# Transposed accumulation for two token tiles of a gated spectral / key-lookup kernel, gate dots later, one more level of minima, a new order

## The chip, the core and the metric

One NeuronCore of a Trainium2 chip runs the kernel. The metric is device microseconds of one launch, the median of a few runs. The engines are TensorE (PE, with its weight loads PEld), VectorE (DVE), ScalarE (ACT), GpSimd (POOL) and the queue of SyncE (SP). All of them share 16 DMA engines.

## What is computed

The input x has 2048 tokens of 576 numbers. Branch a is a spectral filter: a 2-D real FFT, a product with a complex weight, the inverse FFT. Branch b picks, for each token and each of 32 heads, one row out of 4096 by the best of two 64-key scores, and adds up 32 weighted rows of v. A sigmoid gate mixes them.

```python
q  = einsum("nd,dhc->nhc", x, w_q)              # 32 heads, 2*128 numbers
i1 = argmax(q1 @ k1.T); i2 = argmax(q2 @ k2.T)  # 64 keys each, K = 1
e  = i1 * 64 + i2                               # row of u and v, 0..4095
g  = softmax over one candidate                 # = 1
act = gelu(einsum("nd,nhkd->nhk", x, u[e]))
b  = einsum("nhk,nhk,nhkd->nd", g, act, v[e])   # sum of 32 scaled v rows
a  = irfft2(rfft2(x) * (w_r + 1j * w_i))
gate = sigmoid((x * gate_w).sum(-1))
out = gate * a + (1 - gate) * b
```

## The kernel before, in words

The tokens are 16 tiles of 128. The heads are 8 chunks of 4. For each chunk `build_m` (line 335) folds w_q with the keys into a matrix of 512 columns, held in a high and a low part. `scores` (line 362) multiplies it with two token tiles at a time: 28 passes of 128x512 on PE for a pair of tiles, 224 for a chunk, 1792 in all. From the scores in PSUM, DVE takes the maximum of each group of 64 (line 385), ACT makes a sign of every score against its maximum (line 392, 16 instructions for a pair of tiles), and DVE finds the first hit by a tree of minima over bf16 numbers (lines 405, 413, 414) and a last reduction over 16 (line 416). The row number of a token and head goes to `ei` or `eil`.

The first ten tiles (`E_T`, 0 to 9) are worked by `group(t, c)` (line 458). It issues four gathers on POOL (line 465), each of 128 rows of 1152 numbers, u and v side by side, into a buffer `uv`. DVE makes the dot of x and u (line 472), ACT the gelu (line 474), and the factors `a` come from ACT (line 480) or DVE (line 483). The four scaled v rows are then summed in one of these ways, which the table `ROWS` chooses:

- DVE multiplies and adds into the sum `xn` (line 498);
- ACT scales the row in place (line 493), DVE adds it (line 494);
- the whole group goes to PE (an entry of 16): ACT makes four diagonal matrices `dg` (line 508), PE multiplies each with a v row in two halves of 288 columns (line 512), and DVE adds the sum from PSUM (line 522) or ACT copies it (line 520).

The other six tiles (10 to 15) are worked by `quad(t, c)` (line 543) after the last score: their gathers are at line 549, their dots at line 554, and their sums are made on PE with 32-column diagonals. They wait for the score of chunk 7 by `HELD`.

Branch a starts near the end of the scores: `fold` (line 688), then `unit` (line 822) with its twiddle tables from `turns` (line 719), then `invert`, and `mix` (line 868), which adds (1 - gate) times the sum. The gate's dots (`gates`, line 326) stand in two places: those of the first ten tiles near the start, with a copy of gate_w that `spread` (line 588) brings to all partitions by two matmuls, and those of the other six in `close_gates` (line 832), which then makes the sigmoid.

A gather needs a free `uv` buffer. There are 12, and others that come free later: one in `area`, and four `pair` buffers, which hold the x tiles 0 to 7 of the first ten two by two, and become `uv` buffers when the last reader of both x tiles is done (`plan.late`). Four PSUM buffers of two banks (`bank`) go round among scores, `build_m`, diagonal sums and the rest.

Nothing is scheduled by the machine: each piece of work is a job, the list `ORDER` at the end of the file gives the sequence of all jobs, and each engine executes its own in that sequence. An engine whose next job has to wait holds up all that stand behind it.

## Time and profile before

| | |
|---|---|
| median of 3 runs | 894.05 us (890.72 to 895.09) |
| the profiled execution | 895.22 us, its span 893.5 us |
| busy in the span | PE 852.5, PEld 652.8, DVE 822.3, ACT 597.2, POOL 579.5 us |
| moved by DMA | 342.41 MB, of which 302.02 MB are the gathers |
| mean granted TensorE clock | 0.984 |

The profiled execution took 1.7 us more than its span, and 1.2 us more than the median. A busy PE in these views is not PE at its peak, since matmuls overlap; the distance from one start to the next says more. The chain that ended last is the sequence of work that leads back from the last instruction to what released each step.

### The profile page before, as it was taken

The page shows a single profiled execution, that of the slowest core. Times are in us where ns is not written, and L with a number is a line of the kernel's source. Part 1 is how long each engine was busy: PE and PEld are TensorE (multiplying, and loading weights), DVE is VectorE, ACT ScalarE, POOL GpSimd, SP SyncE. Part 2 cuts the span into 40 slices and gives each one's busy share as a digit, 9 for nine tenths or more (in the row PEclk, how much of TensorE's full clock was granted, in tenths as well). Part 3 has the DMA queues.
Part 4 walks back from the last instruction along what each step waited for, and adds up shares of the span by engine and source line. Part 5 has one row for each costly group of instructions (what it writes and reads, how often), then busy time and mean ns, then how long its engine had stood idle before and what let it go on. Part 6 is the DMA issues. An engine that isn't in the chain of part 4 may idle for free.

```text
span 893.5 us, 16499 instructions
## 1 busy us (share of the span) xinstructions
PE 852.5 (95%) x5306; PEld 652.8 (73%) x5306; DVE 822.3 (92%) x2000; ACT 597.2 (67%) x2100; POOL 579.5 (65%) x516
## 2 busy tenths in 40 slices
...
GB/s 301 362 333 407 379 362 363 332 374 382 366 375 393 374 387 357 386 384 367 334 377 364 418 387 371 412 370 416 414 405 415 420 418 419 420 421 419 420 419 305
DMA packets 89611, 342.41 MB, mean 383 GB/s; under 512 B 9970, under 2 KB 10866, under 8 KB 89524
## 3 DMA queue, kind: packets, MB, share of 16 engines
q0 software_dynamic: 73728, 302.02, 86.5%
...
## 4 chain that ended last, share of the span: by engine, by line
PE 61%; DVE 22%; DMA 8%; ACT 5%; issue 3%; POOL 1%; DVEq 0%; SPq 0%; POOLq 0%; ACTq 0%
PE bank L256 61%; DVE uv L472 7%; DMA uv<-uv,ei 4%; DVE xn L498 3%; DVE xn L494 2%; DMA uv<-uv,eiq 2%; DVE area L385 2%; DVE uv L554 2%; ACT area L392 1%; DMA pair<-uv,eiq 1%; ACT uv L493 1%; POOL uv L465 1%; DVE area L405 1%; DVE pair L554 1%; DVE xn L522 0%
## 5 line engine op out<-in xcount | busy, mean ns | idle before, releaser
L465 POOL DMA_INDIRECT uv<-uv,ei x317 | 363.5, 1147 | 214.4 <-issue 44.7
L256 PE MATMUL bank<-mh,xt 128*128 128x512 f32 x768 | 263.3, 398 | 0.0
L392 ACT ACTIVATE area<-bank,area 128x64 bf16<-128x64 f32 x1024 | 222.7, 355 | 21.4 <-DVE area L385 14.4
L472 DVE SCALAR_TENSOR_TENSOR uv<-uv,pair 128x576 f32<-128x576 f32 x254 | 185.8, 751 | 7.9 <-DMA uv<-uv,ei 7.7
L549 POOL DMA_INDIRECT uv<-uv,eiq x136 | 150.3, 1105 | 57.7 <-issue 21.9
L256 PE MATMUL bank<-ml,xt 128*128 128x512 f32 x448 | 174.8, 390 | 0.0
L256 PEld LDWEIGHTS bank<-mh,xt 128*128 128x128 f32 x768 | 144.2, 188 | 31.2 <-ACT area L392 0.3
L256 PE MATMUL bank<-uv,dg 128*32 128x288 f32 (+2 forms) x868 | 146.3, 417 | 14.3 <-DVE dg L558 6.2
L256 PE MATMUL bank<-mhx,xt 128*128 128x512 f32 x384 | 135.2, 400 | 0.0
L256 PEld LDWEIGHTS bank<-uv,dg 128*32 128x32 f32 (+2 forms) x868 | 81.9, 141 | 51.5 <-issue 10.8
L554 DVE SCALAR_TENSOR_TENSOR uv<-uv,xr 128x576 f32<-128x576 f32 x136 | 99.9, 753 | 13.8 <-DMA uv<-uv,eiq 10.7
L256 PE MATMUL bank<-fi,bt 128*128 128x289 f32 x384 | 102.5, 418 | 3.0 <-ACT t L866 1.5
L498 DVE SCALAR_TENSOR_TENSOR xn<-uv,a,xn 128x576 f32<-128x576 f32 x124 | 100.0, 810 | 0.0
L256 PEld LDWEIGHTS bank<-fi,bt 128*128 128x128 f32 x384 | 83.0, 243 | 23.3 <-issue 5.8
L256 PEld LDWEIGHTS bank<-ml,xt 128*128 128x128 f32 x448 | 84.2, 188 | 16.5
L493 ACT ACTIVATE uv<-uv,a 128x576 f32<-128x576 f32 x103 | 77.6, 779 | 12.0 <-DVE a L483 11.8
L256 PEld LDWEIGHTS bank<-mhx,xt 128*128 128x128 f32 x384 | 72.2, 188 | 16.2 <-ACT area L392 0.3
L385 DVE TENSOR_REDUCE area<-bank 128x16 f32<-128x1024 f32 x64 | 77.6, 1216 | 1.5 <-PE bank L256 1.4
L494 DVE TENSOR_TENSOR xn<-uv,xn 128x576 f32<-128x576 f32 x103 | 77.2, 751 | 0.7 <-ACT uv L493 0.7
L256 PE MATMUL bank<-mlx,xt 128*128 128x512 f32 x192 | 74.9, 390 | 0.0
L400 ACT ACTIVATE area<-area 128x256 bf16<-128x256 bf16 x192 | 71.3, 416 | 1.1
L555 ACT ACTIVATE b<-z 128x4 f32<-128x4 f32 x48 | 9.8, 204 | 80.8 <-DVE uv L554 59.5
...
## 6 DMA issues: line engine op xcount, KB each, us to landing
...
uv<-uv,eiq POOLq DMA_INDIRECT x136, 8.5
...
```

Of the source, the lines that this page charges most:

```text
L256: after('PE', nc.tensor.matmul(*args, **kw))
L385: dv(dve(1024, True), lambda: nc.vector.tensor_reduce(mv.ap[:, 2 * tp:2 * tp + 2, :], ps.ap.rearrange('p a (g e) -> p a g e', e=E), AX.X, ...
L392: on('ACT', actv(sg.ap[:, j, g, :], ps.ap[:, j, g * E:g * E + E], AF.Sign, bias=mv.ap[:, 2 * tp + j, g:g + 1], scale=-1.0))
L400: ac(act(256), lambda b=b: actv(s2()[:, :, b * Q:b * Q + Q], s2()[:, :, b * Q:b * Q + Q], AF.Copy, bias=b / 4), [sg], [])
L465: on('POOL', nc.gpsimd.indirect_dma_start(out=g.ap.rearrange('p a d -> p (a d)'), out_offset=None, in_=uv, in_offset=bass.IndirectOffsetOn ...
L472: dv(0.68, lambda k=k, g=rows[k]: stt(g.ap[:, 0, :], g.ap[:, 0, :], 1.0, x.ap, op0=ALU.mult, op1=ALU.mult, accum_out=z.ap[:, k:k + 1]), [( ...
L493: ac(act_by(576), lambda v=v, s=s: actv(v(), v(), AF.Copy, scale=s()), [(rows[k], 1)], [a])
L494: dv(dve(576), lambda v=v: vt(y.ap, v(), y.ap, ALU.add), [y], [(rows[k], 1)])
L498: dv(0.73, lambda v=v, s=s: stt(y.ap, v(), s(), y.ap, op0=ALU.mult, op1=ALU.add), [y], [(rows[k], 1), a])
L549: on('POOL', nc.gpsimd.indirect_dma_start(out=g.ap.rearrange('p a d -> p (a d)'), out_offset=None, in_=uv, in_offset=bass.IndirectOffsetOn ...
L554: dv(0.68, lambda j=j: stt(rows[j].ap[:, 0, :], rows[j].ap[:, 0, :], 1.0, xr[t][j].ap, op0=ALU.mult, op1=ALU.mult, accum_out=z.ap[:, j:j + ...
L555: ac(0.1, lambda: actv(b.ap, z.ap, AF.Gelu_apprx_tanh), [b], [(z, j) for j in range(HPC)], table='gelu')
```

## The change

Seven things are changed.

1. Tiles 0 and 1 (`T_T`) leave the ways above. All their 16 groups go through `lean`: ACT scales the four v rows in place, and PE turns each row in five blocks of 128 columns with `is_transpose` and adds the turned blocks up in one PSUM buffer (`turned`). The first group's sum is copied by ACT to a buffer `xw` of 640 columns, those of the later seven are added by DVE. At the end `mix` turns the sum back, again in five blocks, and adds it to the spectral part in two pieces (512 and 64 columns).
2. The gate dots of the first ten tiles move from the start to `close_gates`. The early copy of gate_w, its matmuls and its load go. The product of a dot is written over the x tile itself, so a tile's dot is now the last reader of x.
3. The tree of minima gets one more level: a minimum over 8 and 8, then a reduction over 8.
4. The first pair of tiles goes through `first`: the two tiles one after the other, each with its own maximum, tree and row numbers.
5. `turns` makes its two transposes with `is_transpose` in place of plain matmuls.
6. The rings change: one `dg` less, two `xn` less and two `xw` instead.
7. `ROWS` has other entries for tiles 2 to 9, and `ORDER` is new. Groups with diagonals on PE are now 13, before 20.

```diff
-    def gates(t, w, junk=None):
+    def gates(t, w, to):
         x = xs[t]
...
+        dv(dve(576), lambda: stt(to.ap[:, :D], x.ap, 1.0, w.ap, op0=ALU.mult, op1=ALU.mult, accum_out=gz[:, t:t + 1]), [('gz', t), to], [x, w])
...
+    def first(ps, mv):
...
+        for j in range(2):
+            dv(dve(512, True), lambda j=j: nc.vector.tensor_reduce(mv.ap[:, j:j + 1, :], ps.ap[:, j:j + 1].rearrange('p a (g e) -> p a g e', e=E), AX.X, ALU.max), [(mv, 0, j)], [(ps, j)])
...
+        dv(0.07 + n * 128 / 1920, lambda: vt(q2()[:, :, :Q // 2], q2()[:, :, :Q // 2], q2()[:, :, Q // 2:Q], ALU.min), keys, [])
+        dv(0.06 + n * 128 / 960, lambda: nc.vector.tensor_reduce(im.ap[:, :2 * n].rearrange('p a h b -> p (a h b)'), q2()[:, :, :Q // 2], AX.X, ALU.min), [im], keys)
...
+    def turned(p, x, first, last):
+        for i in range(ND):
+            lo = i * P if x.shape[1] > D else min(i * P, D - P)
+            mm(p.ap[:, i // 4, i % 4 * P:i % 4 * P + P], x[:, lo:lo + P], ident.bitcast(F32), is_transpose=True, start=first and i % 4 == 0, stop=last and i in (3, 4), skip_group_check=True)
+
+    def lean(t, rows, a):
+
+        pd = psum()
+        for k in range(HPC):
+            v = lambda k=k: rows[k].ap[:, 1, :]
+            ac(act_by(576), lambda k=k, v=v: actv(v(), v(), AF.Copy, scale=a.ap[:, k:k + 1]), [(rows[k], 1)], [a])
+            plan('PE', 0.35, lambda k=k, v=v: turned(pd, v(), k == 0, k == HPC - 1), [pd], [(rows[k], 1), 'ident'])
+        flat = lambda: pd.ap.rearrange('p a b -> p (a b)')[:, :ND * P]
+        if t not in accs:
+            accs[t] = buf('xw', [P, ND * P])
+            ac(act(640), lambda: actv(accs_t.ap, flat(), AF.Copy), [accs[t]], [pd])
+        else:
+            dv(dve(640, True), lambda: vt(accs_t.ap, flat(), accs_t.ap, ALU.add), [accs[t]], [pd])
...
+        if t in T_T:
+            dv(0.08, lambda: vt(a.ap, b.ap, sw[:, t, c * HPC:c * HPC + HPC], ALU.mult), [a], [b, ('sw', t, c)])
+            lean(t, rows, a)
+            return
...
-    gw1 = buf('uv', ROW)
-    spread((gw1, 0), lambda: gw1.ap[:, 0, :])
...
-    for t in E_T:
-        gates(t, gw1)
...
-                mm(flat()[:, n * P:n * P + P], tw.ap[:, n, :], ident.bitcast(F32), start=True, stop=True)
+                mm(flat()[:, n * P:n * P + P], tw.ap[:, n, :], ident.bitcast(F32), is_transpose=True, start=True, stop=True)
...
     def close_gates():
-        jg = psum()
         spread(gw2, lambda: gw2.ap)
+        for t in E_T:
+            gates(t, gw2, xs[t])
         for t in L_SEQ:
-            gates(t, gw2, jg)
+            gates(t, gw2, buf('f5', [P, ND * P]))
...
     def mix(t):
         ga, y = (gas[t], accs[t])
+        if t in T_T:
+            p = psum()
+            plan('PE', 0.35, lambda: turned(p, y.ap, True, True), [p], [y, 'ident'])
...
-ROWS = {0: (0, 16, 16, 15, 6, 2, 14, 2), 1: (4, 15, 0, 13, 5, 16, 7, 16), 2: (12, 4, 2, 16, 10, 8, 16, 1), 3: (0, 10, 14, 9, 0, 7, 1, 16), 4: (6, 9, 0, 2, 16, 2, 16, 14), 5: (2, 0, 15, 16, 12, 9, 12, 16), 6: (2, 15, 4, 8, 16, 6, 16, 14), 7: (0, 4, 16, 16, 5, 0, 5, 2), 8: (4, 16, 7, 5, 13, 16, 16, 4), 9: (12, 14, 13, 16, 7, 0, 16, 11)}
+ROWS = {0: (0, 16, 16, 15, 6, 2, 12, 0), 1: (0, 15, 0, 12, 5, 16, 5, 16), 2: (12, 8, 2, 6, 0, 8, 0, 1), 3: (2, 10, 0, 5, 0, 7, 4, 16), 4: (4, 0, 0, 6, 16, 7, 16, 0), 5: (2, 0, 1, 0, 0, 9, 12, 16), 6: (4, 15, 4, 8, 16, 0, 16, 14), 7: (8, 0, 16, 16, 6, 12, 9, 2), 8: (6, 16, 7, 0, 12, 16, 16, 11), 9: (4, 0, 0, 16, 0, 8, 16, 5)}
...
+T_T = (0,1)
...
-    42, 2, 43, 0, 1, 21, 22, 44, 3, 23, 9, 91, 103, 4, 5, 20, 92, 45, 93, 6, 104, 94, 16, 106, 7, 130, 105, 95, 96, 100, 13, 10, 14, 107, 11, 97, 24,
```

How the instructions move is shown at three places. The first is on PE, between two pairs of score tiles. Before, at the first group that goes to PE (tile 0, chunk 1), there stand the last passes of a score tile, a diagonal sum for each of four rows (`uv` is the v row, `dg` its diagonal), and two passes of `build_m` among them:

```order
L256 MATMUL bank_87<-ml_1012,xt_3_38_514 128x512
L256 MATMUL bank_89<-uv_1551,dg_1691 128x288 x2
L256 MATMUL bank_88<-mh_1714,ident 128x4x64 x2
L256 MATMUL bank_89<-uv_1580,dg_1682 128x288 x2
L256 MATMUL bank_89<-uv_1524,dg_1718 128x288 x2
L256 MATMUL bank_89<-uv_1545,dg_1684 128x288 x2
L256 MATMUL bank_88<-mhx_1282,xt_0_3_154 128x512
```

Now PE has its first such group already in chunk 0 (tile 0), in the middle of a score tile, as four rows of five turned blocks (`ident` is the moving operand):

```order
L260 MATMUL bank_89<-mh_242,xt_2_33_423 128x512
L260 MATMUL bank_88<-ident,uv_575 128x128 x5
L260 MATMUL bank_88<-ident,uv_550 128x128 x5
L260 MATMUL bank_88<-ident,uv_489 128x128 x5
L260 MATMUL bank_88<-ident,uv_503 128x128 x5
L260 MATMUL bank_89<-mhx_213,xt_2_13_477 128x512
```

A group of eight plain matmuls of 288 columns has become twenty turns of 128 columns, and what was on DVE for tile 0 in chunk 0 is on PE.

The second place is on DVE, the sums of tiles 0 and 1. Before, in chunk 0, the dots (with `z`) alternate with a multiply-add or an add for each v row of tile 0 (`xn_712`) and of tile 1 (`xn_759`):

```order
L498 SCALAR_TENSOR_TENSOR xn_712<-uv_516,a_710,xn_712 128x576
L472 SCALAR_TENSOR_TENSOR uv_722,z_738<-uv_722,pair_82 128x576
L483 SCALAR_TENSOR_TENSOR a_757<-b_736,sw 128x4
L494 TENSOR_TENSOR xn_712<-uv_584,xn_712 128x576
L416 TENSOR_REDUCE im_764<-area 128x16
L498 SCALAR_TENSOR_TENSOR xn_712<-uv_512,a_710,xn_712 128x576
L385 TENSOR_REDUCE area<-bank_86 128x16
L498 SCALAR_TENSOR_TENSOR xn_759<-uv_642,a_757,xn_759 128x576
```

Now DVE has for a group of tile 0 (its second) four dots and, where the group before it is summed, one add from PSUM into `xw`:

```order
L523 SCALAR_TENSOR_TENSOR uv_1586,z_1607<-uv_1586,pair_82 128x576
L523 SCALAR_TENSOR_TENSOR uv_1571,z_1607<-uv_1571,pair_82 128x576
L444 TENSOR_TENSOR area<-area,ramp_310 128x32x16
L446 TENSOR_TENSOR area<-area 128x32x8
L447 TENSOR_REDUCE im_1647<-area 128x32
L523 SCALAR_TENSOR_TENSOR uv_1603,z_1607<-uv_1603,pair_82 128x576
L523 SCALAR_TENSOR_TENSOR uv_1613,z_1607<-uv_1613,pair_82 128x576
L435 TENSOR_TENSOR area<-area 128x512
L506 TENSOR_TENSOR xw_86<-bank_91,xw_86 128x640
```

Three or four row-wide instructions for each group have become one, and the new level of the tree (L446) stands between.

The third place is on DVE after the last score, where the gate dots of the late tiles (`gz`) stand among the dots of the quads. Before:

```order
L333 SCALAR_TENSOR_TENSOR bank_86,gz<-xl_6701,t_1148_6788 128x2x288
L558 TENSOR_TENSOR dg_7167<-rp_6210,a_7156 128x128
L498 SCALAR_TENSOR_TENSOR xn_1397<-uv_6909,a_7031,xn_1397 128x576
L333 SCALAR_TENSOR_TENSOR bank_86,gz<-xl_6687,t_1148_6788 128x2x288
L554 SCALAR_TENSOR_TENSOR pair_83,z_7101<-pair_83,xr_6760 128x576
L758 TENSOR_TENSOR t_1194_7182<-bank_88,w_6971 128x578
L333 SCALAR_TENSOR_TENSOR bank_86,gz<-xl_6878,t_1148_6788 128x2x288
L333 SCALAR_TENSOR_TENSOR bank_86,gz<-xl_6710,t_1148_6788 128x2x288
```

Now the dots of the early tiles stand there, on the `pair` buffers that hold their x, and the first quad row in a `pair` buffer comes behind them:

```order
L332 SCALAR_TENSOR_TENSOR pair_85,gz<-pair_85,t_1126_6880 128x576
L609 SCALAR_TENSOR_TENSOR uv_7307,z_7300<-uv_7307,xr_7213 128x576
L775 SCALAR_TENSOR_TENSOR tw_7005<-tq_6804,tw_7005 128x384
L609 SCALAR_TENSOR_TENSOR uv_7290,z_7300<-uv_7290,xr_7227 128x576
L332 SCALAR_TENSOR_TENSOR pair_85,gz<-pair_85,t_1126_6880 128x576
L609 SCALAR_TENSOR_TENSOR uv_7313,z_7300<-uv_7313,xr_7200 128x576
L332 SCALAR_TENSOR_TENSOR pair_83,gz<-pair_83,t_1126_6880 128x576
L611 TENSOR_TENSOR a_7345<-b_7342,lc 128x4
L613 TENSOR_TENSOR dg_7347<-rp_6531,a_7345 128x128
L609 SCALAR_TENSOR_TENSOR uv_7329,z_7350<-uv_7329,xr_7217 128x576
L609 SCALAR_TENSOR_TENSOR uv_7274,z_7350<-uv_7274,xr_7227 128x576
L609 SCALAR_TENSOR_TENSOR pair_84,z_7350<-pair_84,xr_7213 128x576
```

Before, the `pair` buffers served the gathers while the late tiles' gates were made; now they are held until the early tiles' gates are done. In the sequence of gathers the first one into a `pair` buffer was number 302 of 512, and is number 331. In the list of jobs the last score pass stands behind gather number 299 before, and behind number 298 now.

More of the change, by code (lines that the diff above doesn't have):

```diff
@@ L181, in ring @@
         sizes[tag] = n
-    for tag, n in (('cand', 2), ('z', 8), ('b', 8), ('a', 8), ('im', 1), ('fe', 2), ('dg', 4)):
+    for tag, n in (('cand', 2), ('z', 8), ('b', 8), ('a', 8), ('im', 1), ('fe', 2), ('dg', 3)):
         ring(tag, 'sm', n)
     ring('uv', 'gp', NG)
-    ring('xn', 'xp', 2 * NE - 2 * NPAIR)
+    ring('xn', 'xp', 2 * NE - 2 * NPAIR - len(T_T))
     ring('p2', 'ps', 4)
@@ L233, in tile_kernel @@
         plan.opens[f'xe{k}'] = 3 + k
+    for k in range(len(T_T)):
+        fixed['xw', k] = piece(pools['xp'].tile([P, ND * P], F32, tag=f'xw{k}', name=f'xw{k}'), 0, ND * P)
     for n in range(4):
@@ L379, in part @@
             return plan('PE', 0.2275 * len(seq), go, [(ps, j)], list(use.values()))
-        seq = [(j, i) for i in range(ND) for j in range(2)] if tp in (0, 7) else [(j, i) for j in range(2) for i in range(ND)]
+        seq = [(j, i) for i in range(ND) for j in range(2)] if tp in (0, 7) and (c or tp) else [(j, i) for j in range(2) for i in range(ND)]
         js = [part(j, i) for j, i in seq]
@@ L383, in scores @@
         mv = mx[c]
+        if c == tp == 0:
+            first(ps, mv)
+            return
         s = c * 8 + tp
@@ L446, in add_best @@
         mxv = lambda: mv.ap[:, t0:t1, :].rearrange('p t (h a) -> p t h a', a=2)
-        dv(0.1, lambda: vt(to(), mxv()[:, :, :, 0], mxv()[:, :, :, 1], ALU.add), [key], [(mv, tp) for tp in range(t0 // 2, t1 // 2)])
+        dv(0.1, lambda: vt(to(), mxv()[:, :, :, 0], mxv()[:, :, :, 1], ALU.add), [key], [(mv, tp) for tp in range(t0 // 2, t1 // 2)] + [(mv, 0, j) for j in range(2)] * (t0 == 0))
     def soft(cand, to, n, kc, ks):
@@ L528, in repeat @@
         x = xs[t]
-        xr[t] = [buf(('xr', 'xn'), [P, D]) for _ in range(HPC)]
+        xr[t] = [buf(('xr', 'xn', 'xw'), [P, D]) for _ in range(HPC)]
         for h in (0, 2):
```

42 lines of the change are left out of this document (32 added, 10 removed), and 343 rows, old and new, of the table ORDER.

## The prediction

> **What bounds the kernel now.** I read the chain that ended last first, then the windows, then the groups of instructions, then pieces of the timeline for the distance from start to start. The page gives the chain's shares by engine:
>
> ```profile
> PE 61%; DVE 22%; DMA 8%; ACT 5%; issue 3%; POOL 1%; DVEq 0%; SPq 0%; POOLq 0%; ACTq 0%
> ```
>
> PE first, DVE second; but a chain that goes back along a busy engine hides others that are as busy. So I cut the span where the score passes end. In windows for the tile xt alone (PE busy first, count in brackets), all 1792 score passes are in the first two rows; 71.3 us is the end of chunk 0, 551.9 us that of chunk 7:
>
> ```profile
> 0.00:71.30 71.30, 53.40 (x224) 41.62 (x224) 13.34 (x20) 11.23 (x20) 1.00 0.95 335
> 71.30:551.90 480.60, 379.67 (x1568) 290.42 (x1568) 0.00 (x0) 0.00 (x0) 1.00 0.98 375
> ```
>
> The same windows for everything; after the mean come PE, PEld, DVE, ACT and POOL busy, then the granted clock, the DMA share and GB/s:
>
> ```profile
> 0.00:71.30 71.30, 67.19 (x525) 55.00 (x526) 56.79 (x130) 57.50 (x187) 24.31 (x27) 1.00 0.95 335
> 71.30:551.90 480.60, 477.87 (x2934) 388.09 (x2935) 472.90 (x1091) 403.23 (x1513) 320.88 (x279) 1.00 0.98 375
> 551.90:600.00 48.10, 33.64 (x169) 27.15 (x168) 44.17 (x117) 39.43 (x142) 31.34 (x28) 0.82 0.99 381
> 600.00:675.00 75.00, 70.78 (x419) 51.00 (x421) 72.19 (x186) 25.86 (x78) 54.86 (x50) 0.96 1.02 412
> 675.00:860.00 185.00, 181.72 (x1124) 119.83 (x1118) 151.52 (x411) 63.76 (x161) 136.05 (x126) 1.00 1.03 419
> 860.00:893.50 33.50, 21.25 (x152) 11.71 (x148) 24.76 (x70) 7.41 (x22) 12.03 (x10) 0.94 0.86 343
> ```
>
> Two stages. Up to 551.9 us DVE works 529.7 us and is idle 22.2, most of that at the start. After it DMA moves 412 to 419 GB/s, against 375 during the scores: the second stage, 341.6 us long, is set by bytes. DVE has 33 us to spare from 675 us on, but only 2.8 us from 600 to 675, and 3.9 from 551.9 to 600.
>
> How full is PE during the scores? Its busy share doesn't say, starts do:
>
> ```profile
> 13.48 1.15 PE L256 MATMUL bank<-kT,uv 128*64 128x64 f32 x32
> 14.56 0.50 PE L256 MATMUL bank<-mhx,xt 128*128 128x512 f32 x1
> ...
> 40.65 0.61 PE L256 MATMUL bank<-mh,xt 128*128 128x512 f32 x2
> 41.11 0.39 PE L256 MATMUL bank<-ml,xt 128*128 128x512 f32 x1
> 41.33 0.40 PE L256 MATMUL bank<-mh,ident 128*128 128x256 f32 x2
> 41.57 0.40 PE L256 MATMUL bank<-mhx,xt 128*128 128x512 f32 x1
> ...
> 559.75 0.65 PE L256 MATMUL bank<-uv,dg 128*128 128x288 f32 x2
> 560.23 1.28 PE L256 MATMUL bank<-kr,f 128*128 128x128 f32 x10
> ```
>
> From 40.65 to 41.11 two score passes start: 0.23 us each (0.227 over a longer stretch). In the same way a 256-column pass takes 0.12, a 64-column pass of `build_m` 0.034, and a 288-column pass of a diagonal 0.24; a diagonal matmul is two passes in the trace.
>
> ```profile
> L256 PE MATMUL bank<-kT,uv 128*64 128x64 f32 x1280 | 47.8, 232 | 1.4 <-ACT area L392 0.8 <-DVE xn L522 0.6
> L256 PE MATMUL bank<-uv,dg 128*128 128x288 f32 x288 | 75.7, 407 | 1.3 <-ACT dg L508 1.3
> ```
>
> The second row is from the groups of the score stage alone. So PE's work there is 1792 x 0.227 = 406.8, 288 x 0.242 = 69.7, 1280 x 0.034 = 43.5, and 70 passes of 0.12 = 8.4 us: 528 of the 546 us from its first `build_m` at 6.3 us on. DVE and PE are both about 97% full there; DMA is not at its rate. A buffer for the next gather comes free when the engines have used it, so whoever shortens the work of both shortens the stage.
>
> **The change part by part.** Counts are from the order of both kernels up to the last score pass, durations from the trace. For DVE, which overlaps its instructions by some 0.08 us, the pieces of the chain give the share of each, and the groups the counts:
>
> ```profile
> 343.69 2.03 DVE uv L472 x6
> 347.94 0.73 DVE xn L498
> 504.44 1.34 DVE xn L494 x2
> ...
> L494 DVE TENSOR_TENSOR xn<-uv,xn 128x576 f32<-128x576 f32 x93 | 69.6, 750 | 0.0
> L522 DVE TENSOR_TENSOR xn<-bank,xn 128x576 f32<-128x576 f32 x18 | 13.5, 750 | 0.0
> L416 DVE TENSOR_REDUCE im<-area 128x32 f32<-128x512 bf16 x28 | 19.0, 677 | 0.0
> L413 DVE TENSOR_TENSOR area<-area 128x256 bf16<-128x256 bf16 x4 | 1.1, 287 | 0.0
> L416 DVE TENSOR_REDUCE im<-area 128x16 f32<-128x256 bf16 x4 | 1.7, 415 | 0.0
> ```
>
> An add takes 0.67 us, a multiply-add 0.73, a dot with its accumulator 0.68. In the score stage:
> - adds of ACT-scaled rows (L494) 93 to 52: -41 x 0.67 = -27.5 us;
> - adds from PSUM of 576 columns (L522) 18 to 11: -7 x 0.67 = -4.7;
> - the ten gate dots go: -10 x 0.68 = -6.8;
> - multiply-adds (L498) 113 to 123, since tiles 2 to 9 have fewer groups on PE: +10 x 0.73 = +7.3;
> - 13 new adds of 640 columns: 0.67 and 64 columns more, 0.74 as an estimate, +9.6;
> - the first pair's two trees in place of one, an estimate from the 256- and 512-wide rows: +1.5;
> - the new level of minima: 0.287 + 0.415 in place of 0.677, nothing either way (with the overlap off, up to -0.06 each, -1.7 in all).
>
> The sum is -20.6 (to -22) us of DVE's 529.7.
>
> On PE 56 diagonal matmuls of two passes go: -112 x 0.242 = -27.1 us. 300 turns of 128 columns come. No row shows such a turn. From below, 128 columns at the rate of a score pass, 0.227 / 4 = 0.057. From above, if a turn is one pass like those of `fold`, 0.128 (ten passes of 128 columns in 1.28 us); if it is two passes, as a plain 128-column matmul of f32 is here, 0.256. I take 0.07: the turn does no sum of products that needs a second pass, and the nearest row for one pass of f32-wide data is the 512-column one. That is +21 us, PE -6 in all (-10 to +11, or +50 with two passes). The Trainium skill, "TensorE: Matmul & The Clock Gate", Terms, calls the transpose mode four times faster for FP32, which would be, as an estimate, 0.256 / 4 = 0.064 here and -8 us in all; no run so far shows it.
>
> ACT gets 17 scalings more, and 28 diagonals and 28 small factors fewer:
>
> ```profile
> L493 ACT ACTIVATE uv<-uv,a 128x576 f32<-128x576 f32 x103 | 77.6, 779 | 12.0 <-DVE a L483 11.8
> L508 ACT ACTIVATE dg<-ident,a 128x128 f32<-128x128 f32 x80 | 27.6, 391 | 0.1
> L480 ACT ACTIVATE a<-b,sw 128x1 f32<-128x1 f32 x80 | 17.0, 283 | 0.6
> ```
>
> 17 x 0.779 = +13.2, 28 x 0.391 and 28 x 0.283 = -18.9: nothing. ACT has 91 us idle in this stage, which hides it; only in chunk 0, where ACT has 8 of the new scalings (6.2 us) on 57.5 of 71.3 us, is the cover thin. There PE gains 40 turns too (+2.8) and DVE's relief is of no use, since DVE is idle 14.5 us: chunk 0 +1.5 us. The load and matmuls of the early gate_w go, but PE's first `build_m` waits for its own loads: nothing (0 to -0.5).
>
> Chunk by chunk at these prices, the larger of DVE's and PE's work in chunks 1 to 7 is 60.1, 65.8, 64.9, 74.0, 66.8, 67.6, 76.8 before (476.0; the stretch took 480.6), and 59.7, 62.9, 64.1, 68.5, 70.7, 61.6, 74.6 after (462.1): -14. As the two engines are now within 4.5 us of each other in every chunk, and PE's turns wait for ACT's scaling with the next score passes queued behind them, I add 1.5 us of waits. The scores end at 551.9 - 14 + 1.5 + 1.5 = 541 us.
>
> The second stage has as many gathers as before, 213 and 214 of 512, so it does not shrink. What moves there: ten gate dots (+6.8 us of DVE, L333 shows 0.76 for each with the overlap), less five adds and multiply-adds (-3.5), and two mixes in two pieces, one add of 640 and the like (+2.4): +5.7 us of DVE in all.
>
> ```profile
> L333 DVE SCALAR_TENSOR_TENSOR bank<-xl,t 128x576 f32<-128x576 f32 x6 | 4.6, 760 | 0.0
> ```
>
> These dots come about the 331st to 359th gather, which is where DVE has 2.8 us idle from 600 to 675 us: some 2.5 us show. They also hold the four `pair` buffers until some 30 gathers later; 12 to 13 buffers fed 375 GB/s in the scores, so I take +1 (0 to +6) for thinner queues between 552 and 610 us. The turns of `turns` are 18, and cost at most nothing on a PE that isn't the bound. Second stage 341.6 + 3.5 = 345.1.
>
> The span is then 541 + 345.1 = 886.1, 7.4 less than 893.5. The profiled execution took 895.22, 1.2 above the median of 894.05: predicted 886.6, rounded 886.5.
>
> **The rivals.** (a) PE takes the gain: a turn costs 0.128, not 0.07, from the row of `fold`. Then chunks 1 to 7 come to 474.3 (-1.7), chunk 0 gains 40 x 0.128 = 5 us of PE work and ends some 3 us later, and with +3.5 in the second stage it is about 899; at 0.10, about 893: no change. For it: the weights of a turn are the 128 columns of the row itself, loaded anew for each. Against it: nothing in the trace, only the price I chose.
>
> (b) The slower end: a turn is two passes or more. PE's seven chunks come to 507.6 (+31.6), chunk 0 +10 and the second stage +3.5: 939. It decides from about 0.11 us a turn on, where chunks 1 to 7 gain no more than chunk 0 and the second stage lose. For it: the plain f32 transposes of `turns`, 18 matmuls with the identity, are 36 passes in the trace:
>
> ```profile
> L256 PE MATMUL bank<-ident,tw 128*128 128x128 f32 x36 | 6.1, 292 | 0.0
> ```
>
> Against it: the turn is asked for as a transpose, which has nothing to multiply. The Trainium skill, the same page, Part 4, has a rule that speaks for this end: a transpose takes about 275 ns in a kernel, and doesn't count as PE work for the clock. By that, as an estimate, 300 x 0.275 = 82 us come for 27 removed, and the time is some 945 us. The trace has shown a granted clock of 1.00 throughout the scores, with no turn among them.
>
> (c) The second stage gives it back: the 5.7 us of DVE and the late `pair` buffers (+6) cost all they can, 11.7 in place of 3.5. Then 886.5 + 8.2 = 894.7, no change. For it: DVE is 92 to 96% full from 552 to 675 us, and gathers of quads land slowly:
>
> ```profile
> uv<-uv,eiq POOLq DMA_INDIRECT x136, 8.5
> ```
>
> Against it: DMA is at 412 GB/s in the larger part of that stretch, and there is no DVE bound from 675 us on.
>
> (d) All of DVE's saving comes through, since a stage that waits less at its start and has a shorter queue of sums runs even: 551.9 - 20.6, second stage +1: 875.
>
> **How the numbers follow.** Forecast 0.50, its own range 880 to 891; (a) 0.18; (b) 0.07; (c) 0.13; (d) 0.12. The range goes from (d) to the upper end of (a), 874 to 900, and leaves out (b) and the rims of the others. A measurement of this kernel can tell some 0.5% from no change, here 4.5 us: faster is below 889.6, slower above 898.5. Faster is (d) and most of the forecast, 0.12 + 0.44 = 0.56; slower is (b) and a third of (a), 0.13; the rest 0.31.
>
> **What would show it.** Right: last score pass at 538 to 545 us; starts of turns 0.06 to 0.09 us apart; about 52 instructions in the group of ACT-scaled adds before it; DVE still over 94% busy there; a second stage of 342 to 348 us, with its DMA at 415 GB/s from 610 us on. Wrong: turns over 0.11 us apart, a granted clock below 1 in the scores, PE waiting for ACT's scaling by more than some 5 us in all, a chunk 0 that ends after 75 us, or a second stage above 350 us.

## The result, and the profile after

The changed kernel takes 901.33 us (median of 4 runs, 900.38 to 902.42), the kernel before in the same comparison 892.82 (890.72 to 895.09, 4 runs). The ratio is 1.0085, with an interval of 1.0064 to 1.0105: slower by some 8 us. The prediction was 886.5, with faster as the likeliest sign; it was wrong in size and in sign, and 901.33 lies just above its range. The profiled execution took 900.38 us (span 898.6). Ratios and their intervals, here and below, leave out executions that took over 1.5% longer than the fastest of their kernel; the medians take all of them in.

Where the time went is seen best where the prediction cut the span. The windows of the changed kernel for the tile xt alone (PE busy first, count in brackets) show where the score passes end: chunk 0 at 76.8 us, chunk 7 at 554.6 (of 1792 passes in all; one that lies across the cut is counted on both sides).

```profile
0.00:76.80 76.80, 54.84 (x225) 41.27 (x226) 13.69 (x20) 11.51 (x20) 1.00 0.94 338
76.80:554.60 477.80, 385.87 (x1569) 287.91 (x1567) 0.00 (x0) 0.00 (x0) 1.00 0.98 371
```

The same windows for everything (PE, PEld, DVE, ACT, POOL busy, granted clock, DMA share, GB/s), and the second stage in the prediction's pieces:

```profile
0.00:76.80 76.80, 70.02 (x591) 57.93 (x592) 51.84 (x123) 63.36 (x200) 24.53 (x28) 1.00 0.94 338
76.80:554.60 477.80, 477.58 (x3051) 392.87 (x3050) 461.41 (x1095) 395.84 (x1469) 313.55 (x277) 1.00 0.98 371
554.60:600.00 45.40, 32.30 (x184) 27.12 (x183) 41.83 (x113) 35.52 (x126) 26.86 (x25) 0.81 1.01 395
600.00:675.00 75.00, 67.20 (x384) 47.36 (x383) 72.33 (x194) 29.27 (x89) 52.38 (x48) 0.93 1.00 395
675.00:860.00 185.00, 180.35 (x1111) 119.09 (x1110) 153.75 (x417) 62.85 (x158) 138.44 (x125) 1.00 1.02 417
860.00:898.60 38.60, 28.82 (x190) 16.61 (x188) 30.38 (x84) 9.48 (x27) 14.51 (x15) 0.98 0.93 373
```

| stage | before | after | change | forecast |
|---|---|---|---|---|
| chunk 0 | 71.3 | 76.8 | +5.5 | +1.5 |
| chunks 1 to 7 | 480.6 | 477.8 | -2.8 | -12.5 |
| second stage | 341.6 | 344.0 | +2.4 | +3.5 |

VectorE did get lighter: busy 513.3 us to the last score pass in place of 529.7. But its idle time there grew from 22.2 to 41.4 us, 10.5 of that in chunk 0 and 8.7 in chunks 1 to 7. The relief of 16.4 us has become waits.

The price of a turn is in the timeline of PE in chunk 0 (start, busy, instruction, count):

```profile
63.39 0.39 PE L260 MATMUL bank<-ml,xt 128*128 128x512 f32 x1
63.62 0.71 PE L260 MATMUL bank<-ident,uv 128*128 128x128 f32 x5
64.08 0.48 PE L260 MATMUL bank<-mhx,xt 128*128 128x512 f32 x1
64.40 0.39 PE L260 MATMUL bank<-mlx,xt 128*128 128x512 f32 x1
...
66.02 1.80 PE L260 MATMUL bank<-ident,uv 128*128 128x128 f32 x15
67.57 0.47 PE L260 MATMUL bank<-mhx,xt 128*128 128x512 f32 x1
67.89 0.39 PE L260 MATMUL bank<-mlx,xt 128*128 128x512 f32 x1
```

Fifteen turns occupy PE from 66.02 to 67.57, 0.103 us each, and the score pass behind them is followed by the next after 0.32 us in place of 0.23. With that, 15 turns cost 67.89 - 66.02 - 0.227 = 1.64 us, 0.109 each. The block of five gives 64.40 - 63.62 - 0.227 = 0.55 us in the same way, 0.111 each. I use 0.107, a little on the low side: 300 turns are 32 us of PE, where the forecast had 21. PE's work, which was to fall by 6 us, has grown by 5.

The groups of the changed kernel to 554.6 us (busy, mean ns) show one pass for a turn, and the counts that the prediction gave:

```profile
L260 PE MATMUL bank<-ident,uv 128*128 128x128 f32 x300 | 38.8, 272 | 0.0
...
L553 DVE SCALAR_TENSOR_TENSOR xn<-uv,a,xn 128x576 f32<-128x576 f32 x124 | 100.4, 811 | 0.2
L549 DVE TENSOR_TENSOR xn<-uv,xn 128x576 f32<-128x576 f32 x52 | 38.9, 750 | 0.6 <-ACT uv L548 0.5
L447 DVE TENSOR_REDUCE im<-area 128x32 f32<-128x256 bf16 x28 | 11.5, 410 | 0.1
L506 DVE TENSOR_TENSOR xw<-bank,xw 128x640 f32<-128x640 f32 x13 | 10.7, 820 | 1.5 <-PE bank L260 1.5
L577 DVE TENSOR_TENSOR xn<-bank,xn 128x576 f32<-128x576 f32 x11 | 8.2, 750 | 0.1
L446 DVE TENSOR_TENSOR area<-area 128x256 bf16<-128x256 bf16 x28 | 7.9, 283 | 0.1
```

A turn is shown 272 ns long. The Trainium skill, "TensorE: Matmul & The Clock Gate", Part 4, gives about 275 ns for a transpose of bf16 numbers in a kernel: the length agrees for the f32 blocks here, but it isn't what a turn costs. By it, as an estimate, 300 turns would be 82 us. By the distance of their starts they are 32.

Who made DVE wait? The waits of DVE between chunk 0 and the last score (us in total, times, longest), first before, then after:

```profile
DVE uv L472 <- DMA uv<-uv,ei: 6.8, 9, 1.8
DVE area L405 <- ACT area L400: 0.2, 1, 0.2
DVE area L385 <- PE bank L256: 0.2, 1, 0.2
```

```profile
DVE uv L523 <- DMA uv<-uv,ei: 6.9, 8, 3.2
DVE area L415 <- PE bank L260: 2.5, 6, 0.9
DVE a L527 <- ACT b L525: 1.6, 4, 0.7
DVE xw L506 <- PE bank L260: 1.5, 4, 0.5
DVE a L538 <- ACT b L525: 1.3, 3, 0.4
DVE uv L523 <- PE bank L260: 0.6, 1, 0.6
DVE xn L549 <- ACT uv L548: 0.5, 1, 0.5
```

The waits for gathers are the same. New are 8.0 us of waits for PE and ACT, 0.4 before: nearly all of the 8.7.

Chunk 0 is seen in windows from 30 us, when all engines are at work, to the chunk's end. Before:

```profile
30.00:71.30 41.30, 41.30 (x294) 33.68 (x294) 40.70 (x100) 39.04 (x142) 24.11 (x23) 1.00 0.96 342
```

After:

```profile
30.00:76.80 46.80, 46.80 (x362) 38.64 (x361) 37.59 (x98) 46.07 (x158) 24.33 (x24) 1.00 0.98 366
```

DVE was 99% busy there and is 80% busy now; ACT went from 95 to 98%. PE's starts give it 40.8 us of work in the 41.3 before (157 score passes, 131 of `build_m`, 6 of 256 columns) and 45.9 in the 46.8 after (156, 160, 6, and 40 turns). So two engines look full after, PE and ACT, and their busy shares alone don't tell which of them sets the end.

PE's own waits tell more. Between chunk 0 and the last score the kernel before has these:

```profile
PE bank L256 <- ACT dg L508: 1.3, 2, 0.7
PE bank L256 <- ACT area L392: 0.8, 1, 0.8
PE bank L256 <- DVE xn L522: 0.6, 1, 0.6
```

They are 2.7 us in all. For the changed kernel the same view, from 30 us to the last score, has no line: PE works without a gap (46.80 of 46.80 us and 477.58 of 477.80). So 2.7 us of waiting is all that lighter work of the other engines could give back in chunks 1 to 7, and it did; from 30 us on the time of the scores is PE's own work.

### The profile page after: what moved, and what is told of

Same layout as the page of the kernel before. It is cut to its first block, busy times and chain, and to the rows that moved or that the text cites. A ratio compares the mean times of both kernels' runs of the same rounds, so it can differ in the third digit from the quotient of the medians.

```text
span 898.6 us, 16947 instructions
## 1 busy us (share of the span) xinstructions
PE 856.3 (95%) x5502; PEld 661.0 (74%) x5502; DVE 811.5 (90%) x2022; ACT 596.3 (66%) x2067; POOL 570.3 (63%) x516
## 5 line engine op out<-in xcount | busy, mean ns | idle before, releaser
L516 POOL DMA_INDIRECT uv<-uv,ei x317 | 356.6, 1125 | 226.5 <-issue 46.6
L260 PE MATMUL bank<-mh,xt 128*128 128x512 f32 x768 | 269.8, 402 | 0.0
L422 ACT ACTIVATE area<-bank,area 128x64 bf16<-128x64 f32 x1008 | 220.3, 360 | 15.1 <-DVE area L415 10.9
L604 POOL DMA_INDIRECT uv<-uv,eiq x144 | 156.6, 1087 | 70.1 <-issue 23.3
L523 DVE SCALAR_TENSOR_TENSOR uv<-uv,pair 128x576 f32<-128x576 f32 x256 | 187.3, 750 | 12.5 <-DMA uv<-uv,ei 11.9
L260 PE MATMUL bank<-uv,dg 128*32 128x288 f32 (+1 forms) x784 | 115.0, 412 | 4.3 <-DVE dg L613 4.2
L609 DVE SCALAR_TENSOR_TENSOR uv<-uv,xr 128x576 f32<-128x576 f32 x144 | 105.7, 751 | 12.4 <-DMA uv<-uv,eiq 12.1
L553 DVE SCALAR_TENSOR_TENSOR xn<-uv,a,xn 128x576 f32<-128x576 f32 x133 | 107.7, 811 | 0.2
L260 PEld LDWEIGHTS bank<-fi,bt 128*128 128x128 f32 x384 | 82.5, 243 | 20.6 <-issue 6.5
L260 PEld LDWEIGHTS bank<-uv,dg 128*32 128x32 f32 (+1 forms) x784 | 60.6, 131 | 35.7 <-DVE dg L613 10.1
L415 DVE TENSOR_REDUCE area<-bank 128x16 f32<-128x1024 f32 x63 | 76.6, 1217 | 4.3 <-PE bank L260 4.0
L260 PEld LDWEIGHTS bank<-kT,uv 128*64 128x64 f32 x1280 | 41.6, 141 | 18.2 <-issue 13.4
L260 PE MATMUL bank<-kT,uv 128*64 128x64 f32 x1280 | 46.5, 228 | 6.7 <-DMA uv<-wqT 6.7
```

Source lines behind the costliest of these rows:

```text
L260: after('PE', nc.tensor.matmul(*args, **kw))
L415: dv(dve(1024, True), lambda: nc.vector.tensor_reduce(mv.ap[:, 2 * tp:2 * tp + 2, :], ps.ap.rearrange('p a (g e) -> p a g e', e=E), AX.X, ...
L422: on('ACT', actv(sg.ap[:, j, g, :], ps.ap[:, j, g * E:g * E + E], AF.Sign, bias=mv.ap[:, 2 * tp + j, g:g + 1], scale=-1.0))
L516: on('POOL', nc.gpsimd.indirect_dma_start(out=g.ap.rearrange('p a d -> p (a d)'), out_offset=None, in_=uv, in_offset=bass.IndirectOffsetOn ...
L523: dv(0.68, lambda k=k, g=rows[k]: stt(g.ap[:, 0, :], g.ap[:, 0, :], 1.0, x.ap, op0=ALU.mult, op1=ALU.mult, accum_out=z.ap[:, k:k + 1]), [( ...
L553: dv(0.73, lambda v=v, s=s: stt(y.ap, v(), s(), y.ap, op0=ALU.mult, op1=ALU.add), [y], [(rows[k], 1), a])
```

## The experiments

Three theories stood against each other. **A**: TensorE and VectorE are both full in the scores after the change; the turn's price is the main thing that the forecast had wrong. **B**: VectorE alone (or the new order) sets the scores. **C**: TensorE alone does. (The expectations explain their own letters, which are not the same in each.) Of the four chips that the experiments ran on, three took 916 to 927 us for the kernel before (e5, e6 and e7 ran on the other, with 893.87), mainly through a slower second stage (389 GB/s between 610 and 850 us in e11, 411 in the changed kernel's first profile), so kernels are compared by their ratio to the kernel before on the same chip, and by the chunks of kernels that ran together.

### What set the pace before: e4 and e5

e4: the kernel before, its ten early gate dots 64 columns wide.

```diff
-            dv(..., lambda: stt(out_(), two(x.ap), 1.0, two(w.ap[:, 0, :]), ...
+            dv(..., lambda: stt(out_()[:, :, :E // 2], two(x.ap)[:, :, :E // 2], 1.0, ...
```

> The kernel before, with the ten early gate dots over 64 of 576 columns, so those gates are made from part of x: 10 x 0.55 = 5.5 us of DVE less during the scores. If DVE set the pace before, 4 to 5.5 us less than the kernel before (887 to 889 us); if PE did already then, no change (891 to 894 us).

Measured: 922.61 us, ratio 0.9931 (0.9897 to 0.9965). Some 6 us come back (3 to 9 by the interval) for 5.5 us of DVE. Where they come back isn't shown: all ten dots lie in chunk 0, which ends at 71.2 us as before, and no profile of the kernel before was taken on that chip. e5: the kernel before, with one of the four diagonal rows of a group, 52 us of PE less.

```diff
-                for r in range(2):
+                for r in range(2 * (k == 0)):
```

> The kernel before, but of each group that goes to PE only the first of four v rows is multiplied with its diagonal, so these sums leave three rows of four out: 54 rows of 0.97 us, 52 us of PE work less during the scores, nothing less on DVE and ACT. If PE set the pace of the scores before, they get shorter until DVE's 530 us bind: 8 to 20 us less than the kernel before. If DVE did, within 3 us of it.

Measured: 898.07 us, ratio 1.004 (1.0025 to 1.0056); no gain, a small loss. Its windows and the longest waits of PE between 71 and 554 us:

```profile
71.30:554.40 483.10, 443.90 (x2712) 355.05 (x2707) 472.82 (x1089) 402.94 (x1513) 318.33 (x279) 0.97 0.98 373
```

```profile
PE bank L256 <- ACT area L392: 21.7, 14, 2.9
PE bank L256 <- ACT dg L508: 7.7, 7, 2.9
PE bank L256 <- ACT ml L355: 6.4, 4, 2.7
```

PE waits out what it saves, most of it for ACT, while DVE stays 98% busy. So PE was not the only limit of chunks 1 to 7 before the change: without it, DVE and the order of the work hold the stretch at the same length. But PE was as near, with 2.7 us of waits. The prediction's view of two engines that are about equally full holds; its 97% for PE leaves more room than there was.

### What a turn costs in time: e2, e1, e10 and e13

e2: the turns as plain matmuls, two passes each.

```diff
-            mm(..., ident.bitcast(F32), is_transpose=True, start=..., stop=..., ...)
+            mm(..., ident.bitcast(F32), start=..., stop=..., ...)
```

> The changed kernel with the turns of lean and mix as plain matmuls with the identity instead of transposes. By the rows of the plain transposes each turn is then two passes of 0.112 us instead of one of 0.107: 300 turns in the scores cost 35 us of PE more. Theory A: all of it shows, 932 to 940 us, and each chunk grows by its turns (40 turns: 4.7 us in chunk 0). Theory B: PE has some 15 us of idle time to give first, below 922 us.

Measured: 965.55 us, ratio 1.0376 (1.0306 to 1.0447), against 1.0085. On the first comparison's scale that is some 926 us, between the two values that I had expected. From its timeline of PE and its groups to 591.6 us, where its scores end:

```profile
69.61 3.51 PE L260 MATMUL bank<-ident,uv 128*128 128x128 f32 x30
72.88 0.48 PE L260 MATMUL bank<-mhx,xt 128*128 128x512 f32 x1
```

```profile
L260 PE MATMUL bank<-ident,uv 128*128 128x128 f32 x600 | 73.2, 275 | 0.2 <-ACT uv L499 0.2
```

A pass of a plain f32 matmul with 128 columns takes 0.109 us from start to start as well; the transposed form is one pass in place of two, and hardly cheaper for a pass. The second passes are 33 us of PE, and they cost 2.9% of some 927 us, 27 us (20 to 34 by the intervals): PE work added after the change shows for the most part.

e1 takes PE work away: only the first of four rows is turned, 24 us less.

```diff
-            plan('PE', 0.35, lambda k=k, v=v: turned(pd, v(), k == 0, k == HPC - 1), ...
+            plan('PE', 0.35, lambda k=k, v=v: turned(pd, v(), True, True) if k == 0 else None, ...
```

> The changed kernel, but of each group of tiles 0 and 1 PE turns only the first of four scaled v rows; the sums of these tiles leave three rows of four out. 240 of 320 turns go, some 225 of them during the scores, at 0.107 us each: 24 us of PE work less, nothing else less. Theory A (PE sets the pace of the scores: the turns cost 32 us where 27 us of diagonals went, so DVE's 20 us of relief buy nothing): the last score pass comes 14 to 24 us earlier, until DVE's 509 us and its 22 us of idle time bind, and the time is 878 to 888 us. Theory B (DVE or the queue of sums sets the pace, PE only lies beside it): within 3 us of 901. Theory C (the new order, above all in chunk 0, is what costs): chunk 0 keeps its 76 us, the time is above 896.

> The kernel of e1 once more, on another chip: the changed kernel with one of each four rows turned, 75 turns in place of 300, 225 x 0.107 = 24 us of TensorE work less (the rows left out are missing in the sums). Theory A (after the change VectorE and TensorE are equally full in the scores, the turns' price is what the forecast missed): about 10 us faster than the changed kernel, 889 to 892, near the forecast of 886.5; the rest of the 24 us is VectorE's. Theory B (VectorE and the new order alone set the scores): 899 to 902. Theory C (TensorE alone sets them): 877 to 880.

Measured: e1 928.55 us, ratio 0.9964 (0.9919 to 1.001); e10, the same kernel on another chip, 931.15 us, ratio 1.0038 (0.9991 to 1.0086), beside the changed kernel's own 943.33, 1.0128 (1.008 to 1.0176), on that chip (e12). So 24 us of PE work are worth 8 to 11 us, with intervals of some 5 us on either side; e1 missed the 14 to 24 us that I had expected for a PE that sets the pace, and e10 came out between its values. The rest is not there to be had, as the windows of e10 in chunks 1 to 7 show:

```profile
76.40:555.20 478.80, 463.06 (x2855) 372.52 (x2855) 460.92 (x1096) 395.80 (x1469) 313.23 (x277) 1.00 0.98 370
```

DVE's work is as it was, 461 us. In e1 and e10 the stretch takes 479.3 and 478.8 us; in the six kernels of the table below, which have all turns there and ran on such chips, 486.1 to 489.8. So it gets some 8 us shorter, and PE, which waits 7 us there in e12 and not at all in the changed kernel's first profile, waits some 15 us in e10, the most of it for ACT's copies of `build_m` (L347, 6.8 us). So the next limit lies some 8 us behind PE.

e13 sets PE's work to what the forecast had assumed: 195 turns in place of 300.

```diff
-            ... turned(pd, v(), k == 0, k == HPC - 1), ...
+            ... turned(pd, v(), k == 0, k == 2, 3 if k == 1 else ND) if k < 3 else None, ...
```

> The changed kernel with 13 of the 20 turns of each group of four rows (the first and third row whole, three blocks of the second, none of the fourth, so that part of the sums is left out): 195 turns in place of 300. At the measured 0.107 us each that is 20.9 us of TensorE work, as much as the forecast put in for 300 turns at 0.07; all other instructions stay. If the price of a turn is all that the forecast had wrong, this kernel shows the forecast: scores to 541, 886 to 888 in all on a chip on which the changed kernel takes 901. Theory A (price, and beside it a chunk 0 in which TensorE has no gap and waits of two equally full engines): about half of the 11.2 us of TensorE work comes back, 894 to 897, ratio to the kernel before 1.000 to 1.004. Theory B (the new order, whatever a turn costs): 900 to 902, ratio 1.007 to 1.010.

Measured: 919.17 us where the kernel before took 916.17; ratio 1.0001 (0.9957 to 1.0045). That is 0.8% below the changed kernel's first ratio, some 7 us (3 to 12 by the intervals), or half of what separates 901.3 from the forecast; against e17, the changed kernel on the same chip, it is 1.1%. With the price that I forecast the change would have been no change, and not a gain of 0.8%: there is something beside the price.

### How much of VectorE's work still counts: e3, e11 and e7

e3 and e11: the 13 adds from the turned sums 64 columns wide, 8 us of DVE less by my count, 6 in the traces (455 of 462 us in chunks 1 to 7).

```diff
-            dv(dve(640, True), lambda: vt(accs_t.ap, flat(), accs_t.ap, ALU.add), ...
+            dv(dve(640, True), lambda: vt(accs_t.ap[:, :E], flat()[:, :E], accs_t.ap[:, :E], ALU.add), ...
```

> The changed kernel, but DVE's add of a turned sum is 64 columns wide instead of 640, so tiles 0 and 1 keep only 64 columns of their later groups: 13 adds of 0.74 us become some 0.13 us during the scores, 8 us of DVE less, PE unchanged. Theory A: 898 to 902 us, no change. Theory B: 8 us less, 893 us.

> The kernel of e3 once more, on another chip: the changed kernel whose 13 adds of 640 columns from the turned sums are 64 columns wide, some 8 us of VectorE work less (most columns of these sums are left out). Theory A (both engines equally full): 2 to 4 us faster than the changed kernel, 897 to 899. Theory B (VectorE alone sets the scores): 8 us faster, 893. Theory C (TensorE alone): no change, 901.

Measured: e3 935.68 us, ratio 1.0056 (1.001 to 1.0103); e11 940.31 us, ratio 1.0141 (1.0071 to 1.021), beside 1.0128 of the changed kernel. Nothing certain: 0.3% less once, 0.1% more once. In the profiles chunks 1 to 7 take 484.6 us (e3) and 485.7 (e11), 486.1 to 489.8 with the whole adds: some 2 us for 6. Theory B would have all of it: it doesn't fit these stretches, and lies at the rim of what the ratios allow. A and C can't be told apart by these two.

e7: tile 1 goes back to scaled rows that DVE adds, in the places where its turned sums stood; nothing is left out.

```diff
+        if t not in T_U:
...
+                ac(act_by(576), lambda k=k, v=v: actv(v(), v(), AF.Copy, scale=a.ap[:, k:k + 1]), ...
+                dv(dve(576), lambda v=v: vt(y.ap, v(), y.ap, ALU.add), ...
...
+T_U = (0,)
```

> The changed kernel with tile 1 taken out of the turned sums: at the same places in the order ACT scales its rows and DVE adds them, as the kernel before does; tile 0 stays turned. The output is the whole one. PE loses 160 turns (17 us), DVE gets 8 x 4 adds of 0.67 us for 8 adds of 0.74 (15 us more). Theory A: the two engines' sums during the scores are then some 517 and 524 us, the larger of the two is less than in both kernels: 889 to 896 us. Theory B: DVE's 15 us show, 910 to 916 us. Theory C: within 3 us of 901.

Measured: 914.11 us, ratio 1.0231 (1.021 to 1.0251). This missed the 889 to 896 us that I expected. PE's work falls by 16 us, DVE's rises by some 15, and the time by 13. From its windows:

```profile
80.20:570.20 490.00, 471.07 (x2910) 382.70 (x2909) 475.00 (x1116) 396.23 (x1469) 321.55 (x277) 0.99 0.97 364
```

Neither engine is full here: DVE works 475.0 us in 490. To the last score DVE is busy 528.8 us and PE 541.9, no more than in the kernel before (529.7 and 545.1), yet that score comes 18 us later. So it isn't the amount of work that makes e7 slow but waits: PE waits 21 us more than after the change, the longest total being 8.1 us for ACT's copies of `build_m` (L347). Three or four adds stand in one place of an order that was laid out for one; that this is what holds the others up was not tried by itself. So e7 doesn't decide between A and C.

What decides is the profile together with e1, e10 and e2. In the changed kernel as it is, TensorE alone sets the pace: it has no gap (in its first profile; on the slower chips it waits 6 to 7 us in chunks 1 to 7, in e12 and e17), and passes added to it show. C in its full sense, where all of the 24 us would come back, is out with e1 and e10; VectorE, ACT and the order follow close behind, which is what A says.

### What sets chunk 0: e9, e12, e14, e15, e16 and e17

e9 leaves out turns in chunk 0 alone: one of four rows, 3.2 us of PE less. In e1 and e10 these turns are out too. e12 and e17 are the changed kernel itself, each as the measure of its chip.

```diff
+            plan('PE', 0.35, lambda k=k, v=v: turned(pd, v(), k == 0 or c == 0, k == HPC - 1 or c == 0) if k == 0 or c else None, ...
```

> The changed kernel, in which the groups of chunk 0 turn only the first of their four rows: 10 turns of 40 are left there, 30 x 0.107 = 3.2 us of TensorE work less, and nothing else changes (the rows left out are missing in the sums). Theory A (TensorE fills chunk 0 without a gap, so each turn there lengthens it by its own time, and what chunk 0 loses is carried to the end): chunk 0 ends at about 73.6 us in place of 76.8, and the time falls by about 3 us from the changed kernel's, to about 898. Theory B (chunk 0 is longer because of the new order: later gathers, a later start, not because of the turns): chunk 0 stays at 76 to 77 us and the time at 901.

> The changed kernel itself, as a measure for the three others on the same chip: 901, within 1 us, by every theory; the chunks as in its first profile (chunk 0 to 76.8 us, scores to 554.6) within 1 us.

e14 makes ACT's scalings in chunk 0 narrow, e15 does both, e16 makes all 64 scalings narrow.

```diff
+        w = 8 if c == 0 else D
...
+            ac(act_by(576), lambda k=k, v=v: actv(v()[:, :w], v()[:, :w], AF.Copy, scale=a.ap[:, k:k + 1]), ...
```

> The changed kernel, in which ScalarE scales only 8 of 576 columns of each turned v row in chunk 0 (8 instructions; the rest of these rows stays unscaled, so their sums are off): some 8 x 0.5 = 4 us of ScalarE less before chunk 0 ends, nothing else changes. Theory A (from 30 us on TensorE and ScalarE are both full in chunk 0): less of one alone brings 0 to 1.5 us; chunk 0 ends 0 to 1.5 us before that of the changed kernel on this chip. Theory B (ScalarE alone sets chunk 0): 3 to 4 us earlier. Theory C (TensorE alone): no change.

> As the kernel before it, and in chunk 0 only one of four rows is turned as well: 4 us of ScalarE and 30 x 0.107 = 3.2 us of TensorE less there (scaling and rows left out in these sums). Theory A (both full): chunk 0 ends 3 to 4 us earlier than in the changed kernel on this chip, more than with either alone. Theory B (ScalarE alone): the same 3 to 4 us as without the turns left out. Theory C (TensorE alone): the same 2 us as with the turns alone left out. D (the order of the work, neither engine): within 1 us of the changed kernel.

> The changed kernel with all 64 scalings of turned rows 8 columns wide in place of 576 (sums off by the scaling), some 64 x 0.5 = 32 us of ScalarE less in the scores. If ScalarE counts in chunk 0 alone, as one of two full engines there, 0 to 2 us less in all. If turns that wait for their scaling hold up TensorE in chunks 1 to 7 (1.5 us of waits in the forecast), 3 to 6 us less.

> The changed kernel itself, as a measure for the three others on the same chip: chunk 0 to 76.8 us within 1 us, scores to 554.6 within 1 us on an undisturbed chip and up to 567 on one like that of the last such run; ratio to the kernel before 1.006 to 1.013.

Chunk 0 and the scores, in each one's profiled execution; the first two ran together, and the last four:

| kernel | less in chunk 0 | chunk 0 ends | scores end | ratio |
|---|---|---|---|---|
| e12 | nothing | 77.8 | 566.6 | 1.0128 (1.008 to 1.0176) |
| e9 | 3.2 us of PE | 75.7 | 562.6 | 1.01 (1.0017 to 1.0183) |
| e17 | nothing | 77.5 | 564.0 | 1.011 (1.005 to 1.017) |
| e14 | 4 us of ACT | 77.3 | 567.1 | 1.0136 (1.0074 to 1.0198) |
| e15 | both | 74.8 | 560.9 | none |
| e16 | 4 us of ACT (32 in all) | 78.3 | 564.4 | 1.0067 (1.0028 to 1.0106) |

(e12 itself missed the expected 901 us, since the kernel before took 926.74 there. e15 has no ratio; its 12 runs have a median of 932.12 us, e17's six 937.0.) The whole-program ratios are too wide to decide here; the chunk's own end does. In windows to the end of chunk 0, e17, e14 and e15:

```profile
0.00:77.50 77.50, 70.86 (x591) 58.62 (x592) 51.62 (x123) 63.80 (x201) 25.27 (x28) 1.00 0.93 336
```

```profile
0.00:77.30 77.30, 70.72 (x591) 58.62 (x592) 51.69 (x123) 60.55 (x201) 25.93 (x28) 1.00 0.93 336
```

```profile
0.00:74.80 74.80, 68.64 (x561) 55.83 (x562) 50.87 (x121) 58.62 (x198) 24.48 (x28) 1.00 0.94 340
```

ACT is 3.3 us lighter in e14, and the chunk ends 0.2 us earlier; with 30 turns less as well it ends 2.7 earlier, against the 2.1 that the turns alone gave in e9. One execution of each is little, since the chunk's end scatters: with all 40 turns it comes at 76.6 to 78.3 us in eight profiles (the changed kernel, e3, e6, e11, e12, e14, e16, e17), without 30 of them at 74.8 to 76.4 in four (e1, e9, e10, e15). The two groups lie apart, by 1.9 us in the mean for 3.2 us of PE. So PE sets chunk 0; ACT, though 98% busy, doesn't. But ACT is next: in e9 PE has a wait that the changed kernel doesn't have, and e15, whose ACT is lighter too, doesn't have it either:

```profile
PE bank L260 <- ACT area L422: 1.3, 1, 1.3
```

e1 and e10 show it as well, with 1.1 and 1.2 us. It accounts for most of what is missing from 3.2, and for e9's chunk ending 2.1 us earlier where I had expected some 3.

Of e16's 32 us of ACT 0.4% comes back, some 4 us, which would fit turns that wait for their scaling; but the intervals overlap, and its scores end no earlier (564.4 and 564.0 us). No sign beyond the noise that PE waits for the scalings.

### The second stage: e6

e6 makes the 16 late gate dots 64 wide.

```diff
-        dv(dve(576), lambda: stt(to.ap[:, :D], x.ap, 1.0, w.ap, ...
+        dv(dve(576), lambda: stt(to.ap[:, :E], x.ap[:, :E], 1.0, w.ap[:, :E], ...
```

> The changed kernel with all 16 late gate dots over 64 of 576 columns, so the gates are made from part of x: 16 x 0.55 = 9 us of DVE less between some 604 and 650 us, nothing less during the scores. My step in the prediction (ten dots cost some 2.5 us there, since DVE is nearly full) makes it 2 to 5 us less than the changed kernel, 896 to 899 us. If DMA alone sets the second stage: no change, 900 to 902 us.

Measured: 899.42 us, ratio 1.0063 (1.0041 to 1.0085), about 2 us below the changed kernel's with overlapping intervals, at the lower end of the 2 to 5 us that I had expected; its second stage is 343.0 us. From the groups behind the last score, after and in e6:

```profile
L332 DVE SCALAR_TENSOR_TENSOR pair<-pair,t 128x576 f32<-128x576 f32 x8 | 5.8, 749 | 0.0
```

```profile
L332 DVE SCALAR_TENSOR_TENSOR pair<-pair,t 128x64 f32<-128x64 f32 x8 | 1.6, 220 | 0.0
```

All 16 dots come to 8.5 us less of DVE, and 1 to 2 us of time: most of this work is hidden, as forecast.

## Why the prediction was wrong, step by step

- **Two engines that are equally full before the change: right, but PE had less room than was said.** PE's passes were summed to 528 of 546 us, 18 to spare. Its waits in chunks 1 to 7 were 2.7 us, and in chunk 0 from 30 us on there were none. So a lighter DVE could give back 2.7 us there and no more, unless PE's own work fell; it rose. e5 shows that relief of PE alone brought nothing either.
- **DVE's counts and prices: right, the sum slightly large.** 52 scaled adds, 11 adds from PSUM, 13 of 640 columns at 0.82 us shown (0.74 with the overlap), 283 + 410 ns of minima for 677. Busy time fell by 16.4 us where 20.6 to 22 were said. Some 2 of the missing 4 us are a term that the sum left out: `lean` makes the 16 factors `a` of the turned groups on DVE, where the sum only took small factors from ACT.

```profile
L527 DVE TENSOR_TENSOR a<-b,sw 128x4 f32<-128x4 f32 x16 | 2.5, 158 | 2.0 <-ACT b L525 1.9
```

  One more multiply-add (124 for 123) is 0.7 us; the rest was not taken apart.
- **The price of a turn: wrong, and the step that cost most.** I took 0.07 "from the nearest row for one pass of f32-wide data", the 512-column score pass, and scaled by columns. It is 0.107 to 0.111, nearer to the other bound, the 0.128 of `fold`, than to 0.07. That turned PE's -6 us into +5. With 0.107 the larger of DVE's and PE's work in chunks 1 to 7 sums to 468.8 instead of 462.1 (the prediction's 474.3 for 0.128, less 260 turns x 0.021): 6.7 of the 9.7 us that are missing there. e13 measures the price alone at some 7 us.
- **Waits of two engines that are equally full: wrong in kind.** I said 1.5 us more. The stretch exceeds the sum of its larger works by 9.0 us (477.8 - 468.8), before by 4.6, but PE has no waits in it. The 9.0 us are PE work that the prices leave out: score passes next to `build_m` are 0.32 and 0.34 us from the next start, in place of 0.23.

```profile
99.17 0.39 PE L260 MATMUL bank<-ml,xt 128*128 128x512 f32 x1
99.39 0.39 PE L260 MATMUL bank<-mh,xt 128*128 128x512 f32 x1
99.71 1.15 PE L260 MATMUL bank<-kT,uv 128*64 128x64 f32 x32
100.79 0.50 PE L260 MATMUL bank<-mh,xt 128*128 128x512 f32 x1
101.13 0.39 PE L260 MATMUL bank<-ml,xt 128*128 128x512 f32 x1
```

  28 such blocks in chunks 1 to 7, at 0.2 us each, are some 5 to 6 us; the rest was not taken apart. Before the change they were there too, but hidden in part, where DVE's work was the larger. The waits of DVE for PE and ACT, from 0.4 to 8.0 us, are what a DVE that is no longer the limit has to wait.
- **PE waits for ACT's scaling: not seen.** I named it as the wait to fear; the group of turns shows no idle time before it, and e16 gains nothing certain.
- **Chunk 0: wrong, +5.5 for +1.5.** I counted 40 turns as +2.8 us and let half of it show, since PE was not taken for full there. It was: 40.8 us of work in 41.3. On PE the turns are 4.1 us, score passes 1.1 more (part of it the 0.09 us after each block of turns), the later start 0.4 (its first `build_m` at 6.7 us, before at 6.3). ACT's thin cover, which I had named, was not the cause (e14); it limits what less PE work would bring (e9).
- **The second stage: right,** +2.4 for +3.5, with 417 GB/s from 675 us on.
- **The rivals.** It went by (a): PE takes the gain. By its own line from 0.10 (893) to 0.128 (899), 0.107 would be about 894.5; the chunk 0 term and the unpriced PE work add the rest. I gave it 0.18, since I had weighed only the price of a turn and not that PE had no room left to be wrong in. (b) decided "from about 0.11": the slower side was that near, and I looked for it only at two passes. The Trainium skill, "TensorE: Matmul & The Clock Gate", Terms, gives the transpose mode a factor of four for FP32; against the plain form in e2, 0.218 for two passes, the factor here is two.

Put together, the scores end 2.7 us later: PE has 5 us more to do (32 for turns, 27 less for diagonals) and starts 0.4 us later, and the 2.7 us that it waited are gone.

What stays open: the rest in DVE's sum and in the 9.0 us, which limit lies behind PE in chunks 1 to 7 (DVE, ACT's copies, the order), and how much of e7's loss is the order. No version tried beats the kernel before with the whole computation.
